# Columns of 1 + ca by one-column products, and one more pair of products of ones

## The chip, the cores and the metric

The kernel runs on one core of one Trainium2 chip. The metric is the device time of one execution in microseconds (us), the median of several runs. A core has TensorE (PE, with its weight loads listed apart as PEld), VectorE (DVE), ScalarE (ACT), GpSimd (POOL) and SyncE (SP), which here issues the DMAs. TensorE multiplies a loaded 128x128 block of weights with a stream of columns and writes into PSUM; the other engines read PSUM or SBUF.

## The reference

One block on x of 2048 rows by 512 columns, with a condition vector c of 512 numbers:

```python
mod = (silu(c) @ w_mod).reshape(1, 6, 1, -1)          # sa, ca, ga, sb, cb, gb: 512 numbers each
h = layernorm(x) * (1 + ca) + sa
x = x + ga * A(h)      # linear attention: 32 heads of 16, phi(q), phi(k), num / den, times wo
h = layernorm(x) * (1 + cb) + sb
x = x + gb * B(h)      # gelu(h @ w_in), halves z1 and z2, (w_sp @ layernorm(z2) + b_sp) * z1, times w_out
```

## The kernel before, in words

The rows are tiles of 128 (16 of them), the 512 columns four chunks of 128 (`KC`). Large products run on numbers split in two (`hi`, `lo`), three products for one. Three stages follow each other: q, k, v and the sums of the attention; the attention's output, the second layer norm and the gelu; and the product with w_sp, where seven products take the place of eight.

The order of all work is written out by hand as a string of short operation names with arguments (`ORDER`, `ORDER3`), and each engine takes its own instructions in that order. Which buffer a tile gets is written out too, as one digit for each allocation of a pool (`SLOTS`); a tile waits until the last user of its buffer is done.

The change is in the first few microseconds. There the layer norm's scale and shift are folded into the weights. For that the kernel needs 1 + ca in two forms. `col` (line 207) has it as one column for each chunk. `cbr` (line 326) has it divided by 512 and repeated along 128 columns, as the weights of a product that gives, for w_k and w_q, the mean of every column of the scaled weight matrix (`wm`, line 332). VectorE then forms the scaled weights less their mean (`wf`, line 336), ScalarE and VectorE or GpSimd split them (`wk`, `wq`, lines 340 and 343), and the first products of k (`kp`, line 417) start.

The operations at the start, in the order's names:

- `lm1,kc` loads chunk kc of w_mod for ca (`raw_mod`), `lw1,h` and `lw0,h` load the halves of w_k and w_q (`raw_qkv`), `ly` loads transposed x (`xt`); SyncE issues them all.
- `si` is silu(c) on ScalarE and VectorE: `sil`, 128x4.
- `du` is two products of a 128x128 tile of ones with itself (`warm`, line 172), whose result nobody reads.
- `cm1,kc` (`col_mm`) is four products with w_mod as weights and silu(c) as the streamed operand, into PSUM `pcol` (line 194).
- `mc` (`mean_col`) is ScalarE's copy from `pcol` to `cbr`; `ce1` (`col_end`) the one to `col`.
- `mr1,kc` and `mr0,kc` (`mean_mm`) are the mean products of w_k and w_q.

In the part that the diff leaves alone stands a product of another kind that the prediction uses: `col_part`, whose `pcol` (line 201) streams one column of ones.

Of the kernel before, what the change touches and what calls it, by code (L numbers as in the profile page):

```python
# [10 lines left out]
AF = mybir.ActivationFunctionType  # L11
# [3 lines left out]
P = 128  # L15
S, D, H, FH = 2048, 512, 32, 688
NT = S // P
KC = D // P
# [8 lines left out]
def block_kernel(ctx: ExitStack, tc: tile.TileContext, x, x_t, w_qkv, w_o, w_in, w_sp, b_sp, w_out,  # L27
                 w_out_tail, c, w_mod, ident_c, mask_c, out):
    nc = tc.nc

    def pool(name, bufs, space=None, stack=None):
        if space is None:
# [28 lines left out]
        "psb": "101010101010101010010101010101001010101",  # L61
        "zs": "0fe123d4cba9876523d483ca9473b2dca74b2dc724d9b7c9dbc9dbc9dbc90fe165d83a4270b9cfe8234",
        "tb": (
            "065412360541631520641326542362361232134614206320606346536132613136256106313012161350420435610253"
            "2564424054541321414101110331614101212465063563"
        ),
        "pst": "01011010101110101",
        "st": "032102312302102310232020312031320121302030132031231302032130210321032103132030211302210130132103",
        "ws": "0101",
        "pso": "010101001001110101011010110100101010010101010101",  # L70
        "tq": "nedc012mlba9876543kjgfihnea1m209ih60598l4k3bjca02inh16",
        "z1": "0000000000000000",
        "u": "0101101010101010",
        "c1": "0000000",
# [5 lines left out]
    def slot(tag):  # L80
        n = turn[tag] = turn.get(tag, -1) + 1
        return f"{tag}.{SLOTS[tag][n]}"

    def sb(tag, shape, dt, name):
        return pools[tag].tile(shape, dt, tag=slot(tag), name=name)

    def ps(kind, shape, name):
        return {"b": psb, "t": pst, "o": pso}[kind].tile(shape, F32, tag=slot("ps" + kind), name=name)
# [16 lines left out]
    mm = nc.tensor.matmul  # L105
# [30 lines left out]
    RAW = {}  # L136
# [37 lines left out]
    sil = const.tile([P, KC], F32, name="sil")  # L174
# [10 lines left out]
    MY, CP = {}, {}  # L185
# [2 lines left out]

    def col_mm(m, kc):
        if m not in CP:  # L190
            CP[m] = ps("t", [P, KC, P], f"pcol{m}")
        for i in range(KC):
            n = NCOL[m] = NCOL.get(m, 0) + 1
            mm(CP[m][:, i], RAW["mod", m, kc // 2][:, kc % 2, i * P:(i + 1) * P],
               sil[:, kc:kc + 1].to_broadcast([P, P]), start=n == 1, stop=n == KC * KC, skip_group_check=True)

    def col_part(key):
        CP[key] = ps("t", [P, KC], f"pcol{key}")
# [4 lines left out]

    def col_end(key):
        COL[key] = const.tile([P, KC], F32, name=f"col{key}")
        p = CP[key][:, :, 0] if key == 1 else CP[key]
        nc.scalar.activation(COL[key], p, AF.Copy, bias=1.0 if key == 1 else 0.0)

    def mod_vec(m, lo=0, hi=KC):
# [112 lines left out]
    WC, WF = {}, {}  # L322

    def mean_col():
        WC["c"] = sb("tb", [P, KC, P], F32, "cbr")
        nc.scalar.activation(WC["c"], CP[1], AF.Copy, scale=1.0 / D, bias=1.0 / D)

    def mean_mm(j, kc):
        if j not in WC:
# [208 lines left out]
    def win_lo(h, kc, eng=nc.gpsimd):  # L538
# [4 lines left out]
    OPS = {  # L543
        "lx": load_x, "lw": load_w, "lm": load_m, "li": load_ident, "du": lambda k: dummy(2), "si": silu,
        "ly": load_xt, "lk": load_wk, "s1": s1, "bh": s2_hi, "bl": s2_lo, "cm": col_mm, "cr": col_part, "ce": col_end,
        "mc": mean_col, "mr": mean_mm, "wf": w_mid,
        "cv": lambda: (col_part("v"), col_end("v")), "mv": lambda m, k: mod_vec(m, k, k + 1), "vp": v_prod, "va": v_add,
        "th": turn_hi, "tl": turn_lo,
        "by": bias_part, "bp": bias_prod, "ba": bias_add, "bx": bias_split, "bb": bias_row, "be": bias_end,
# [230 lines left out]
    def hx_lo(t):  # L780
# [13 lines left out]
        "l5": lambda: load_mod(5, "s4"),  # L794
    })
    ORDER = """
        lm1,0 lm1,1 si du1 du2 du3 du4 cm1,0 lm1,2 cm1,1 cm1,2 lm1,3 cm1,3 mc lw1,0 du5 mr1,0 mr1,1 ly1 th1
        tl1 ce1 lw1,1 mr1,2 mr1,3 ly0 th0 tl0 ly2 th2 wf1,3 qh1,3 qg1,3 lw0,0 tl2 lw0,1 wf1,1 mr0,0 mr0,1
        qh1,1 qg1,1 mr0,2 wf1,0 qh1,0 lx0 mr0,3 lm0,1 s10 yp0,1 ki1,3 ki1,1 lm0,0 yp0,0 ki0,3 ki0,1 ki0,0
        kj0,1 wf1,2 lm0,2 yp0,2 ki1,0 kj1,1 lm0,3 bh0 kj0,3 qh1,2 kj1,3 ki1,2 ly5 qd1,0 wf0,0 wf0,1 wf0,3  # L800
        ya0,1 kj1,0 yp0,3 ya0,2 ya0,3 ki0,2 qh0,1 qd1,2 th5 kj1,2 qh0,0 qg0,0 kj0,0 lx1 kj0,2 lx2 s12 bh2 cr0
# [380 lines left out]
```

## Time and profile before

| what | us |
|---|---|
| three runs | 619.77, 620.29, 621.38 |
| median | 620.29 |
| profiled execution | 620.6 |
| its span in the trace | 618.8 |

A fp32 product stands in the trace as two passes, each a weight load and a matmul; the written order counts products. A pass is shown from its issue to its modelled end, which lies behind the issue of the next one, so the pace is the distance between starts. In the timeline a row is: start, length, engine, line, operation, written tile <- read tiles, shapes, count, and in brackets the idle time ahead of it with what ended it. Rows that follow each other on an engine are merged. In the windows a row is: the stretch, its length, busy time of PE, PEld, DVE, ACT and POOL with the number of instructions, the granted clock of TensorE, the DMA share and GB/s.

### The profile page before, as it was taken

The numbers are of one execution on the slowest core, as the hardware profiler recorded it, in microseconds if no ns is written. First come the engines' busy times: TensorE is split into PE (matmuls) and PEld (weight loads), VectorE is DVE, ScalarE is ACT, GpSimd is POOL, SyncE is SP. The second block draws the span as 40 slices with busy tenths as digits, with TensorE's granted clock in tenths as the row PEclk, the third lists the DMA queues.
The fourth block names the chain that finished last, engine by engine and source line by source line (L and its number), as shares of the span: only waits on it lengthen the run. The fifth ranks groups of instructions, "written<-read, shape, count | busy, mean of one in ns | idle before, by whom it ended". The sixth has DMA issues, their size and how long they took to land.

```text
span 618.8 us, 9545 instructions
## 1 busy us (share of the span) xinstructions
PE 613.3 (99%) x3387; PEld 560.3 (91%) x3387; DVE 487.0 (79%) x902; ACT 336.1 (54%) x580; POOL 224.0 (36%) x185
## 2 busy tenths in 40 slices
PE   9999999999999999999999999999999999999997
PEld 6788888888899999999999999999999999998886
DVE  2999889897788878787786799997767787887661
ACT  2876767565656667565536464454354453544320
POOL 0843444637666576464252420132112111300000
PEclk9999999999999999999999999999999999999999
DMA  8463323261244667566844965552496555989962
GB/s 297 162 191 118 105 68 103 83 194 37 64 122 120 163 175 190 169 199 176 201 138 161 355 217 132 203 168 73 155 199 211 154 182 145 287 267 253 295 223 81
DMA packets 91022, 105.74 MB, mean 171 GB/s; under 512 B 57088, under 2 KB 57600, under 8 KB 90976
## 3 DMA queue, kind: packets, MB, share of 16 engines
q1 hardware_dynamic: 90976, 105.15, 57.2%
q8 instruction: 26, 0.43, 0.3%
q14 instruction: 20, 0.16, 0.1%
HBM read 66.07 MB, written 25.95 MB: 149 GB/s over the span
## 4 chain that ended last, share of the span: by engine, by line
PE 69%; DVE 14%; DMA 7%; issue 5%; POOL 2%; ACT 2%; SPq 1%; POOLq 0%; DVEq 0%; ACTq 0%
PE z L659 15%; PE P L937 13%; PE pout L111 3%; PE pout L112 3%; PE pout L110 3%; DMA raw_wsp<-in_w_sp 3%; PE g L110 2%; PE g L112 2%; PE qp L112 2%; PE qp L111 2%; PE qp L110 2%; PE g L111 2%; PE kp L110 2%; PE po L112 2%; PE kp L111 2%
## 5 line engine op out<-in xcount | busy, mean ns | idle before, releaser
L659 PE MATMUL z<-win,ht 128*128 128x344 f32 x768 | 123.0, 320 | 0.2 <-DVE ht L298 0.2
L659 PEld LDWEIGHTS z<-win,ht 128*128 128x128 f32 x768 | 121.4, 188 | 1.2 <-DVE ht L298 0.5
L937 PE MATMUL P<-z,f 128*128 128x344 f32 x624 | 103.3, 320 | 0.4 <-DVE f L927 0.4
L937 PEld LDWEIGHTS P<-z,f 128*128 128x128 f32 x624 | 99.1, 188 | 0.9 <-DVE f L927 0.7
L927 POOL TENSOR_TENSOR f<-raw_wsp,f 128x512 fp32r<-128x512 f32 x26 | 37.9, 1467 | 138.4 <-ACT f L924 132.1
L254 POOL TENSOR_TENSOR mv<-ve,mhalf 128x1 f32<-128x1 f32 x48 | 35.4, 740 | 54.9 <-DVE ve L253 52.5
L924 ACT ACTIVATE f<-raw_wsp 128x512 fp32r<-128x512 f32 x52 | 31.8, 626 | 29.9 <-PE P L937 14.1
L924 ACT ACTIVATE f<-sa 128x512 fp32r<-128x512 f32 x39 | 24.2, 629 | 33.2 <-DVE sa L914 10.1
L477 POOL TENSOR_TENSOR pksum<-pksum,tk 128x512 f32<-128x512 f32 x15 | 23.1, 1538 | 41.4 <-DVE tk L449 34.2
L927 DVE TENSOR_TENSOR f<-sa,f 128x512 fp32r<-128x512 f32 x39 | 28.5, 741 | 9.6 <-ACT f L924 9.6
L111 PE MATMUL pout<-wout,ut 128*128 128x512 f32 (+1 forms) x85 | 32.2, 379 | 0.2 <-DVE wout L1063 0.2
L110 PE MATMUL pout<-wout,ut 128*128 128x512 f32 (+1 forms) x85 | 32.2, 379 | 0.0
L112 PE MATMUL pout<-wout,ut 128*128 128x512 f32 (+1 forms) x85 | 32.2, 379 | 0.0
L695 POOL TENSOR_TENSOR z<-zz,z 128x688 fp32r<-128x688 f32 x16 | 29.2, 1842 | 7.5 <-ACT z L692 7.5
L937 PE MATMUL Pq<-z,wsp 128*128 128x344 f32 x192 | 30.8, 321 | 0.0
L937 PEld LDWEIGHTS Pq<-z,wsp 128*128 128x128 f32 x192 | 30.6, 188 | 0.0
L1032 ACT ACTIVATE ut<-ur 128x384 fp32r<-128x384 f32 x32 | 15.2, 518 | 24.8 <-DMA ur<-ud 15.8
L268 ACT COPY uca<-us 128x768 uint16<-128x768 uint16 x32 | 25.0, 828 | 5.3 <-PE P L937 3.6
L588 POOL TENSOR_TENSOR prod<-pq,zrep 128x512 f32<-128x512 f32 x16 | 21.7, 1370 | 14.5 <-ACT zrep L714 4.2
L110 PE MATMUL po<-m,pt 128*128 128x512 f32 x64 | 25.3, 396 | 0.0
L112 PE MATMUL po<-m,pt 128*128 128x512 f32 x64 | 25.3, 396 | 0.0
L110 PE MATMUL g<-pkhl,hhl 128*128 128x512 f32 x64 | 25.3, 395 | 0.0
(260 smaller groups left out, 1557.8 us busy)
## 6 DMA issues: line engine op xcount, KB each, us to landing
raw_wsp<-in_w_sp SPq DMA_DIRECT2D x32, 512.0 KB, 4.7
ud<-uca SPq DMA_DIRECT2D x16, 384.0 KB, 3.3
ur<-ud SPq DMA_DIRECT2D x16, 384.0 KB, 4.2
z1d<-z SPq DMA_DIRECT2D x16, 344.0 KB, 2.3
zd<-zz SPq DMA_DIRECT2D x16, 344.0 KB, 2.7
z1r<-z1d SPq DMA_DIRECT2D x16, 344.0 KB, 4.1
xt<-in_x_t SPq DMA_DIRECT2D x16, 256.0 KB, 3.0
x<-in_x SPq DMA_DIRECT2D x16, 256.0 KB, 2.9
```

The costliest lines, as they stand in the source:

```text
L110: mm(o, a_hi, b_hi, start=first, stop=False, **kw)
L111: mm(o, a_hi, b_lo, start=False, stop=False, **kw)
L112: mm(o, a_lo, b_hi, start=False, stop=last, **kw)
L254: nc.gpsimd.tensor_tensor(mv[:, 1:2], ve, mhalf, op=OP.pow)
L268: nc.scalar.copy(pl[:, h], v[:, :, h])
L477: nc.gpsimd.tensor_add(pksum, pksum, PK[t])
L588: nc.gpsimd.tensor_mul(pr, PQ[t], KV["z"])
L659: mm(p[:, b, :HB], a[:, i, kc], win[h][:, j, kc, b * HB:(b + 1) * HB], start=kc == 0 and k == 0, stop=kc == KC - 1 and k == 2)
L695: nc.gpsimd.tensor_sub(Z2[t][:, 1], ZZ[t], f(Z2[t][:, 0]))
L924: nc.scalar.activation(SF[p, h, k][:, 0], s_src(p, h, k), AF.Copy)
L927: eng.tensor_sub(SF[p, h, k][:, 1], s_src(p, h, k), f(SF[p, h, k][:, 0]))
L937: mm(B[key][:, :HB], a[:, x_], b[:, y_], start=i == 1, stop=i == n)
```

## The change

The 16 column products stream one column of silu(c) instead of the same column 128 times, and write a PSUM tile of 128x4 instead of 128x4x128. ScalarE's copy to `cbr` reads each of the four columns 128 times. In the order, `du6` is put behind `du5`: two more products of ones, four passes. In the buffer tables `tb` and `tq` a few digits change places (that of `tb`, two rows long, is left out below).

```diff
-            CP[m] = ps("t", [P, KC, P], f"pcol{m}")
+            CP[m] = ps("t", [P, KC], f"pcol{m}")
         for i in range(KC):
             n = NCOL[m] = NCOL.get(m, 0) + 1
-            mm(CP[m][:, i], RAW["mod", m, kc // 2][:, kc % 2, i * P:(i + 1) * P],
-               sil[:, kc:kc + 1].to_broadcast([P, P]), start=n == 1, stop=n == KC * KC, skip_group_check=True)
+            mm(CP[m][:, i:i + 1], RAW["mod", m, kc // 2][:, kc % 2, i * P:(i + 1) * P],
+               sil[:, kc:kc + 1], start=n == 1, stop=n == KC * KC, skip_group_check=True)
...
-        p = CP[key][:, :, 0] if key == 1 else CP[key]
+        p = CP[key]
         nc.scalar.activation(COL[key], p, AF.Copy, bias=1.0 if key == 1 else 0.0)
...
-        nc.scalar.activation(WC["c"], CP[1], AF.Copy, scale=1.0 / D, bias=1.0 / D)
+        nc.scalar.activation(WC["c"], CP[1][:, :, None].to_broadcast([P, KC, P]), AF.Copy, scale=1.0 / D, bias=1.0 / D)
...
-        "tq": "nedc012mlba9876543kjgfihnea1m209ih60598l4k3bjca02inh16",
+        "tq": "nedc012fgba9876543kjmlihnea1f209ih60598g4k3bjca02inh16",
...
-        lm1,0 lm1,1 si du1 du2 du3 du4 cm1,0 lm1,2 cm1,1 cm1,2 lm1,3 cm1,3 mc lw1,0 du5 mr1,0 mr1,1 ly1 th1
-        tl1 ce1 lw1,1 mr1,2 mr1,3 ly0 th0 tl0 ly2 th2 wf1,3 qh1,3 qg1,3 lw0,0 tl2 lw0,1 wf1,1 mr0,0 mr0,1
+        lm1,0 lm1,1 si du1 du2 du3 du4 cm1,0 lm1,2 cm1,1 cm1,2 lm1,3 cm1,3 mc lw1,0 du5 du6 mr1,0 mr1,1 ly1
+        th1 tl1 ce1 lw1,1 mr1,2 mr1,3 ly0 th0 tl0 ly2 th2 wf1,3 qh1,3 qg1,3 lw0,0 tl2 lw0,1 wf1,1 mr0,0 mr0,1
```

On TensorE the start of the program reads, before (a count is of products):

```order
L172 MATMUL warm<-ones 128x128 x8
L194 MATMUL pcol_182<-sil,raw_mod_0_166 128x128 x8
L194 MATMUL pcol_182<-sil,raw_mod_1_187 128x128 x8
L172 MATMUL warm<-ones 128x128 x2
L332 MATMUL wm_208<-raw_qkv_0_204,cbr 128x512 x2
L332 MATMUL wm_208<-raw_qkv_1_218,cbr 128x512 x2
L332 MATMUL wm_242<-raw_qkv_0_235,cbr 128x512 x2
```

And now:

```order
L172 MATMUL warm<-ones 128x128 x8
L194 MATMUL pcol_182<-sil,raw_mod_0_166 128x1 x8
L194 MATMUL pcol_182<-sil,raw_mod_1_187 128x1 x8
L172 MATMUL warm<-ones 128x128 x4
L332 MATMUL wm_210<-raw_qkv_0_204,cbr 128x512 x2
L332 MATMUL wm_210<-raw_qkv_1_220,cbr 128x512 x2
L332 MATMUL wm_244<-raw_qkv_0_237,cbr 128x512 x2
```

The two more products of ones stand ahead of the first mean products of w_k; the first `wm` is that of w_k, the second that of w_q. No other instruction has another place, on TensorE or on any other engine or queue. What the buffers' change moves is waits. On VectorE, where the scaled w_q is formed, before (with the engine or queue whose semaphore a row waits for):

```order
L343 TENSOR_TENSOR wk<-wf_248,wk 128x512 [waits Activation_49]
L336 SCALAR_TENSOR_TENSOR wf_303<-raw_qkv_0_235,col_216,wm_242 128x512 [waits DMAHW2_49,PE_49]
L336 SCALAR_TENSOR_TENSOR wf_305<-raw_qkv_0_235,col_216,wm_242 128x512 [waits Pool_49]
L336 SCALAR_TENSOR_TENSOR wf_307<-raw_qkv_1_238,col_216,wm_242 128x512 [waits DMAHW3_49,DVE_49]
L343 TENSOR_TENSOR wk<-wf_283,wk 128x512 [waits Activation_49]
```

And now:

```order
L343 TENSOR_TENSOR wk<-wf_250,wk 128x512 [waits Activation_49]
L336 SCALAR_TENSOR_TENSOR wf_305<-raw_qkv_0_237,col_218,wm_244 128x512 [waits DMAHW2_49,PE_49,Pool_49]
L336 SCALAR_TENSOR_TENSOR wf_307<-raw_qkv_0_237,col_218,wm_244 128x512
L336 SCALAR_TENSOR_TENSOR wf_309<-raw_qkv_1_240,col_218,wm_244 128x512 [waits DMAHW3_49,DVE_49]
L343 TENSOR_TENSOR wk<-wf_285,wk 128x512 [waits Activation_49]
```

The wait for GpSimd has moved up by one instruction, from `wf01` to `wf00`. The other changed pairs are `ek1` and `tk1` in the first stage, one z1 tile and one zz tile of the second, and buffers of `tq` in the third.

More of the change, by code (lines that the diff above doesn't have):

```diff
@@ L63, in block_kernel @@
         "tb": (
-            "065412360541631520641326542362361232134614206320606346536132613136256106313012161350420435610253"
-            "2564424054541321414101110331614101212465063563"
+            "065412365041631025641326042362361232134614256325656340630132013130260150313512101365425436015263"
+            "2604424654541321414161116331014161212405603503"
         ),
```

## Prediction

> **What bounds the kernel now.** I read the page first, then the chain of waits from its start, then the timeline of TensorE over the first 24 us, which is all that the change touches.
>
> ```profile
> PE 613.3 (99%) x3387; PEld 560.3 (91%) x3387; DVE 487.0 (79%) x902; ACT 336.1 (54%) x580; POOL 224.0 (36%) x185
> ...
> PE 69%; DVE 14%; DMA 7%; issue 5%; POOL 2%; ACT 2%; SPq 1%; POOLq 0%; DVEq 0%; ACTq 0%
> ```
>
> TensorE is busy for nearly the whole span and holds most of the chain. What is lost ahead of its long run of products therefore comes back as time, and the question is what sets the start of that run. The chain of waits in order of time says it (start, length, what):
>
> ```profile
> 5.67 8.57 DMA raw_qkv<-in_w_qkv
> 14.24 0.14 issue
> 14.38 3.67 PE wm L332 x8
> 18.05 5.58 PE kp L417 x24
> ```
>
> The first half of w_q lands at 14.24 and releases the mean products of w_q (`wm` at 14.38); right behind them come the first products of k (`kp`). What TensorE does before 14.38 is off the chain, as long as it is done by then. The timeline of the engines (start, length, engine, line, operation, count) shows what that is:
>
> ```profile
> 0.98 3.78 PE L172 MATMUL warm<-ones 128*128 128x128 f32 x16 [0.98 <-POOL tiny L124]
> 4.81 4.94 PE L194 MATMUL pcol<-sil,raw_mod 128*128 128x128 f32 x32
> 9.58 0.61 PE L172 MATMUL warm<-ones 128*128 128x128 f32 x4
> 9.78 0.60 ACT L326 ACTIVATE cbr<-pcol 128x512 f32<-128x512 f32 x1 [7.18 <-PE pcol L194]
> 10.43 3.70 PE L332 MATMUL wm<-raw_qkv,cbr 128*128 128x512 f32 x8 [0.24 <-ACT cbr L326]
> 14.38 3.67 PE L332 MATMUL wm<-raw_qkv,cbr 128*128 128x512 f32 x8 [0.24 <-DMA raw_qkv<-in_w_qkv]
> ```
>
> Each fp32 product is two passes in the trace, so two products per `du` are four passes. In order: 16 passes of ones, 32 column passes (`pcol`), 4 passes of ones beside ScalarE's copy `cbr`, 8 mean passes for w_k, 8 for w_q. The mean passes of w_k end at 14.13 by the row (10.43 + 3.70); with 0.592 us for a pass the last one starts at 13.54, and 0.429 later (their pace, below) TensorE could take the next, at 13.97. The slack before 14.38 is 0.4 us.
>
> The pace of the passes is the second thing to see. Three narrow windows of the timeline, with the tile view's lines for the two kinds of column passes behind them (min/median/max ns):
>
> ```profile
> 1.79 1.49 PE L172 MATMUL warm<-ones 128*128 128x128 f32 x6
> ...
> 5.58 1.70 PE L194 MATMUL pcol<-sil,raw_mod 128*128 128x128 f32 x7
> ...
> 7.80 1.39 PE L194 MATMUL pcol<-sil,raw_mod 128*128 128x128 f32 x11
> ...
> 11.82 1.88 PE L332 MATMUL wm<-raw_qkv,cbr 128*128 128x512 f32 x4
> ...
> L194 PEld LDWEIGHTS pcol<-sil,raw_mod x32: 190/191/333, 4.8 to 9.4; 128*128 128x128 f32 x32
> L194 PE MATMUL pcol<-sil,raw_mod x32: 273/273/554, 4.8 to 9.5; 128*128 128x128 f32 x32
> L201 PEld LDWEIGHTS pcol<-ones,yp x8: 187/192/192, 23.5 to 24.2; 128*128 128x128 f32 x8
> L201 PE MATMUL pcol<-ones,yp x8: 250/250/272, 23.5 to 24.3; 128*128 128x1 f32 x8
> ```
>
> A pass lasts longer than its distance to the next one, so I take the last pass off and divide by one less than the count. With 0.42 us for a slow pass, the second row gives (1.70 - 0.42) / 6 = 0.213 us; the third, with 0.273, gives 1.117 / 10 = 0.112; the fourth, with 0.592, 1.288 / 3 = 0.429. Passes of one form became 1.9 times as fast at about 7.2 us, in the middle of the `pcol` row, with no wait ended there. The granted clock stands in the windows at 1.00 from the start, so the opening has to be read from the durations; its closing does stand there:
>
> ```profile
> 614.00:616.00 2.00, 1.69 (x15) 1.48 (x13) 0.38 (x2) 0.00 (x0) 0.00 (x0) 1.00 0.19 66
> 616.00:618.00 2.00, 0.00 (x0) 0.00 (x0) 0.15 (x1) 0.00 (x0) 0.00 (x0) 1.00 0.19 66
> 618.00:618.80 0.80, 0.00 (x0) 0.00 (x0) 0.00 (x0) 0.00 (x0) 0.00 (x0) 0.60 0.00 0
> ```
>
> The last matmul ends at 615.69 (1.69 busy after 614.00). A mean of 0.60 over the last 0.80 us is 0.16 us at 1.0 and the rest at 0.5, so the clock fell at 618.16, about 2.5 us after the work stopped. TensorE thus begins at half speed, opened here 6.2 us after the first full-width pass (0.98 to 7.2), and answers idleness after 2.5 us.
>
> **The change part by part.** *One-column passes, if the clock is granted as before.* Each of the 32 passes streams 1 column where it streamed 128, but loads the same 128x128 weights. The kernel has such passes already:
>
> ```profile
> 23.47 1.05 PE L201 MATMUL pcol<-ones,yp 128*128 128x1 f32 x8
> ```
>
> (1.05 - 0.25) / 7 = 0.114 us apart, against 0.112 for the wide ones; the weight load bounds both (191 and 192 ns). So nothing is gained: the columns end at 9.6 or 9.7 as before. Even passes at no cost would gain nothing on the chain, since the 14.24 of w_q does not move: no DMA is moved, and the queue of SP has the same rows in the same order.
>
> *ScalarE's copy with a repeated source.* 128x512 written as before, at 0.60 us. The trace has no copy that reads one PSUM column 128 times. The nearest row is the copy itself; if it took twice as long, `cbr` would come at 10.98 and the w_k means would end 0.6 us later, 0.2 us past the slack. Faster by half would gain nothing. I take 0.
>
> *`du6`, four passes.* 4 x 0.112 = 0.45 us at full clock. The passes then run from 9.58 to 10.48, where `cbr` is there at 10.38 and the means began at 10.43: 0.05 us, inside the slack of 0.4. At half speed the eight take 8 x 0.213 = 1.7 us, and they stand ahead of the means on TensorE's queue.
>
> *Buffers.* In `tb` the tiles `wf00` and `wf01` change places, so that `wf00` now reuses the buffer whose last reader is GpSimd's second `wk` subtraction.
>
> ```profile
> 15.66 2.54 POOL L343 TENSOR_TENSOR wk<-wf,wk 128x512 fp32r<-128x512 f32 x2 [14.66 <-ACT wk L340]
> 19.08 2.06 DVE L336 SCALAR_TENSOR_TENSOR wf<-raw_qkv,col,wm 128x512 f32<-128x512 f32 x3
> ```
>
> That reader is done at 18.20 and `wf00` starts at 19.08: 0, with 0.9 us of cover. The other swaps in `tb` and `tq` are of pairs that follow each other closely; no engine's order moves. 0.
>
> *The clock, if one-column passes do not count toward it.* Between the ones that end at 4.56 and `du5`, TensorE would then do no work that the gate sees. The trace cannot price this directly: its only one-column stretch is 1 us long with the clock long open. I work it out from the rows above. The 32 passes stay at 0.213 (the slow weight load's 333 ns against 191 keeps that pace): 4.81 + 32 x 0.213 = 11.63. `du5` and `du6`: 1.7, to 13.33. `cbr` is done before that (last pass over at 11.84, plus 0.60 = 12.44). The w_k means start at 13.33 with a pass of 0.429 x 1.9 = 0.82 until the clock opens, 0.429 after. Full-width work began again at 11.63. The lower end for the opening is the gate's quick answer of 2.5 us, at 14.1; the upper end is the opening that the trace shows, 6.2 us, at 17.8. In the first case one pass is slow and seven are fast: the means end at 17.2. In the second 5.5 are slow: 18.9. The w_q means follow without a wait, as w_q has landed long before; against 14.38 that is +2.8 or +4.5 us. Where the gate stood in its cycle in this execution is one draw, so I take the middle, an opening at 16.0: 3.3 slow passes, 4.7 x 0.429 = 2.0, end at 18.0, **+3.7 us**.
>
> Nothing behind takes it back: the chain runs on from `wm` to `kp`, VectorE's `wf` and GpSimd's subtractions wait for the same means, and the later loads wait for buffers that these free. The 24 `kp` passes on the chain are 5.58 / 24 = 0.233 us apart, so there is no stall among them that could shrink in return.
>
> The Trainium skill, "TensorE: Matmul & The Clock Gate", Part 1 (The HAM clock gate), puts the gate's look at 3413 ns windows that run freely of the kernel; the trace agrees with that, 618.16 - 7.2 being 179.0 such windows. By that figure, as an estimate from the page, the first full window behind 11.63 ends 3.4 to 6.8 us later, which would give +3.2 to +4.8 us instead. The Trainium skill, the same page, Part 4 (PE-mode transpose), says that transposes do not count as PE-busy in the same way; no run here shows what a one-column pass counts as.
>
> Sum: 0 + 0 + 0 + 0 + 3.7. The profiled execution took 620.6 (span 618.8 and 1.8 around it), so 624.3. The median of the three runs is 620.29, 0.3 lower, and would give 624.0; I keep 624.3.
>
> **The rivals.**
>
> *The gate counts every pass.* Then the clock opens near 7.2 and all terms are 0 or hidden: 620.6, between 620.3 and 620.9. For it: TensorE and its weight load are both shown busy without a gap over one-column passes, and a weight load moves as much data as before. Against it: the array multiplies one column of 128. The point that decides is whether the 32 passes fall from 0.213 to 0.112 us within the `pcol` row. The Trainium skill, "TensorE: Matmul & The Clock Gate", Part 1, has the gate watch how busy TensorE is, which read plainly gives this case.
>
> *The gate opens early, on the first ones, and closes again.* The 16 passes of ones last 3.6 us; with another position of the gate's cycle that may do. The columns then run fast, the clock falls before the means, and opens again between 13 and 15 us: w_k's means from 10.4 have 3.2 to 5.6 slow passes and end between 15.1 and 16.0, +0.7 to +1.6 us, some 621.8. Against it: in this execution the ones alone did not open it.
>
> *Faster.* Columns that end early would let w_k's means start when w_k lands. But w_q's landing at 14.24 holds what follows, and behind it stand only the 0.14 us of issue: 620.5 at best. To pass 0.3%, w_q's means would have to start at 12.5, before their data are there. Only an effect far behind that I do not see, of the swapped buffers, does that.
>
> **How the numbers follow.** The clock withheld: 0.55. Every pass counts: 0.28. Opens and closes again: 0.10. Faster: 0.07. A measurement of this kernel tells about 0.3% (1.9 us) from no change. Slower is the first case and a third of the third, 0.58; same is the second with the rest of the third, 0.35; faster 0.07. The likeliest case alone spans 623.1 to 625.1. Since the second and third cases hold too much to leave out, the range reaches down to them, and half a microsecond further for the scatter of the runs shown (619.77 to 621.38): 619.8 to 625.4.
>
> **What would show it.** Right: `pcol` passes 0.21 us apart to the end, `pcol` over near 11.6, eight passes of ones to 13.3, the first means 0.8 us apart, w_q's means starting between 17 and 19 with no DMA wait, and the chain at the start running over TensorE instead of w_q's transfer. Wrong: passes 0.11 us apart after some 7 us and `wm` for w_q still at 14.4. What would upset all of it is a wait that the buffer swaps add far behind, or a slow repeated copy of well over 1 us.

## The result, and the profile after

The changed kernel takes 626.50 us (median of 8 runs, 622.35 to 627.27) against 620.33 of the kernel before beside it: a ratio of 1.0081, 95% interval 1.0063 to 1.0099. It is slower, by 5.0 us (3.9 to 6.1) as the ratio gives it; the medians alone lie 6.2 us apart. Its runs spread over 5 us where those of before spread over 1.7. The profiled execution is one of the quicker ones: 624.17, span 622.0.

The page after shows where in the span the clock is missing. These are its first slices of the granted clock, and the chain by engine:

```profile
PE 616.0 (99%) x3391; PEld 561.8 (90%) x3391; DVE 487.7 (78%) x902; ACT 335.6 (54%) x580; POOL 223.2 (36%) x185
...
PEclk7999999999999999999999999999999999999999
...
PE 83%; DVE 5%; DMA 5%; issue 3%; POOL 2%; ACT 1%; SPq 0%; POOLq 0%; DVEq 0%; ACTq 0%
```

The first slice has seven tenths; before, it read nine. The timeline of TensorE and ScalarE's copy, after (start, length, engine, line, operation, count):

```profile
4.79 1.92 PE L194 MATMUL pcol<-sil,raw_mod 128*128 128x1 f32 x16
6.88 2.48 PE L194 MATMUL pcol<-sil,raw_mod 128*128 128x1 f32 x16 [0.17 <-DMA raw_mod<-in_w_mod]
9.22 2.06 PE L172 MATMUL warm<-ones 128*128 128x128 f32 x8
9.40 0.60 ACT L326 ACTIVATE cbr<-pcol 128x512 f32<-128x512 f32 x1 [6.79 <-PE pcol L194]
11.07 8.95 PE L332 MATMUL wm<-raw_qkv,cbr 128*128 128x512 f32 x16
```

And the windows of the same execution (stretch, length, busy PE, PEld, DVE, ACT, POOL, granted clock, DMA share, GB/s):

```profile
4.70:8.00 3.30, 3.10 (x27) 2.98 (x27) 0.00 (x0) 0.00 (x0) 0.00 (x0) 1.00 0.89 258
8.20:14.80 6.60, 6.60 (x19) 4.53 (x20) 1.39 (x2) 2.55 (x5) 0.00 (x0) 0.50 1.03 405
15.00:20.00 5.00, 5.00 (x13) 2.23 (x12) 3.34 (x6) 1.93 (x4) 1.88 (x2) 1.00 1.02 385
```

Here the ones alone opened the clock: the first 16 one-column passes already come (1.92 - 0.25) / 15 = 0.111 us apart. Then it fell while TensorE was busy with one-column passes, between 8.0 and 8.2, and came back between 14.8 and 15.0. The 16 mean passes follow each other without a break, since w_q has long landed. The last ends at 20.02 where it was 18.05 (14.38 + 3.67) before: 2.0 us. The repeated copy takes 0.60 us as before.

That is not the whole loss. If each product of TensorE is laid beside the same product of before, the delay is 2.4 to 2.5 us from 26 us on and stays so until 380 us; it is 4.2 at 385 and 3.2 at the end. The step lies in the third stage, where the change reaches only by buffer numbers. Windows at that place, before and then after:

```profile
380.00:390.00 10.00, 10.00 (x65) 10.00 (x65) 9.09 (x20) 3.78 (x8) 2.55 (x2) 1.00 0.84 228
```

```profile
380.00:390.00 10.00, 8.87 (x54) 8.29 (x53) 9.86 (x21) 5.64 (x11) 0.19 (x1) 1.00 0.57 151
```

TensorE, busy without a gap before, lacks 1.1 us of work there, and VectorE is now the engine with hardly a gap. In the waits from 340 to 400 us, before and then after, TensorE waits for VectorE's `f`:

```profile
PE P L937 <- DVE f L927: 0.2, 1, 0.2
```

```profile
PE P L937 <- DVE f L927: 1.0, 1, 1.0
```

VectorE in turn starts on the tiles `e` late, before and then after:

```profile
346.79 1.98 DVE L873 TENSOR_TENSOR e<-e 128x344 f32<-128x344 f32 x1
```

```profile
351.92 0.52 DVE L873 TENSOR_TENSOR e<-e 128x344 f32<-128x344 f32 x1 [2.60 <-DMA e<-zd]
```

SyncE's queue shows why these tiles come late. Before:

```profile
342.68 0.32 SPq L688 DMA_DIRECT2D zd<-zz  x1
343.10 0.38 SPq L868 DMA_DIRECT2D e<-zd  x1
343.53 0.45 SPq L868 DMA_DIRECT2D o<-zd  x1
```

After:

```profile
345.14 0.32 SPq L688 DMA_DIRECT2D zd<-zz  x1
348.80 0.32 SPq L868 DMA_DIRECT2D e<-zd  x1
349.17 0.42 SPq L868 DMA_DIRECT2D o<-zd  x1
```

The first load of `e` (the third stage's z tiles) comes 0.42 us behind the last store of `zz` before, and 3.66 us behind it after.

So there are two theories. The clock theory: one-column passes do not count toward TensorE's clock. The buffer theory: the swapped tables hold back the loads of the third stage. Rivals are that the four more passes are the loss (queue theory), and that the step at 380 us only follows from the shift at the start.

### The profile page after: what moved, and what is told of

It is laid out like the page before. It is cut to its first block, busy times and chain, and to the rows that moved or that the text cites. A ratio compares the mean times of both kernels' runs of the same rounds, so it can differ in the third digit from the quotient of the medians.

```text
span 622.0 us, 9549 instructions
## 1 busy us (share of the span) xinstructions
PE 616.0 (99%) x3391; PEld 561.8 (90%) x3391; DVE 487.7 (78%) x902; ACT 335.6 (54%) x580; POOL 223.2 (36%) x185
## 4 chain that ended last, share of the span: by engine, by line
PE 83%; DVE 5%; DMA 5%; issue 3%; POOL 2%; ACT 1%; SPq 0%; POOLq 0%; DVEq 0%; ACTq 0%
PE P L937 22%; PE z L659 16%; PE Pq L937 5%; PE pout L111 3%; PE pout L110 3%; PE pout L112 3%; PE g L110 2%; PE g L112 2%; PE qp L112 2%; PE qp L111 2%; PE qp L110 2%; PE g L111 2%; PE kp L110 2%; PE po L112 2%; PE kp L111 2%
```

## The experiments

**Wide products again, all else as changed.**

```diff
-            CP[m] = ps("t", [P, KC], f"pcol{m}")
+            CP[m] = ps("t", [P, KC, 128], f"pcol{m}")
...
-               sil[:, kc:kc + 1], start=n == 1, ...
+               sil[:, kc:kc + 1].to_broadcast([P, 128]), start=n == 1, ...
...
-        nc.scalar.activation(WC["c"], CP[1][:, :, None].to_broadcast([P, KC, P]), ...
+        nc.scalar.activation(WC["c"], CP[1][:, :, 0:1].to_broadcast([P, KC, P]), ...
```

> Everything of the change but the narrow products: the column products stream 128 columns again, ScalarE still copies one of them 128 times, du6 and the swapped buffer tables stay. Clock theory (one-column passes do not count toward TensorE's clock): no loss is left, 620.3 as before, within 0.7 us; the pace doubles once near 4.7 to 8 us and the clock stays open; w_q's means start near 14.4. Buffer theory (part of the loss, the 0.7 to 1.2 us that the changed kernel's trace shows from 381 us on, is from the swapped tables): 621.0 to 621.5, with that step at 381 us again. Queue theory (the four more passes are the loss): 624 to 627.

Measured: 623.11, ratio 1.0034 (1.0018 to 1.0049), 2.1 us. The start of its timeline:

```profile
4.60 4.91 PE L194 MATMUL pcol<-sil,raw_mod 128*128 128x128 f32 x32
9.34 1.05 PE L172 MATMUL warm<-ones 128*128 128x128 f32 x8
10.23 3.66 PE L332 MATMUL wm<-raw_qkv,cbr 128*128 128x512 f32 x8
14.46 2.81 PE L332 MATMUL wm<-raw_qkv,cbr 128*128 128x512 f32 x6 [0.57 <-DMA raw_qkv<-in_w_qkv]
```

The start is whole again: w_q's means wait for w_q. `du6` and the copy are hidden, as the prediction had them. But 2.1 us are lost, and TensorE's delay, under 0.3 us up to 380, is 1.7 us at 385. Neither the clock theory alone (620.3) nor the queue theory (624 to 627) has that; the buffer theory has, with about twice its number (0.7 to 1.2 us).

**Narrow products and copy alone**, with du5 alone and the tables of before.

```diff
-        ... cm1,3 mc lw1,0 du5 du6 mr1,0 mr1,1 ly1
+        ... cm1,3 mc lw1,0 du5 mr1,0 mr1,1 ly1
...  the tables tb and tq as before the change
```

> The narrow products and the repeated copy alone: no du6, the buffer tables of before. Clock theory: the loss stays, 622 to 627 with a median 0.4 to 0.9 us under the changed kernel's, since four slow passes (0.85 us) are gone ahead of w_k's means but the clock opens no earlier. Buffer theory: 1 us or more under the changed kernel's. Queue theory: 620.3 as before.

Measured: 623.75, ratio 1.0050 (1.0032 to 1.0068), 3.1 us. The queue theory falls. The loss without the tables is 2 us under that of the whole change, more than the four passes explain.

**64 columns in place of one.** The first diff with 64.

> The changed kernel with 64 streamed columns in place of 1 (128 before); the weight load still sets the pace, so the passes come at the same distance. If the clock goes by the time in which the array is streamed through, a pass counts half here: either that is enough (620.3, pace doubled once and kept) or it is not (622 to 627, as with one column). I expect it not to be enough to open the clock but enough to keep it open, so some runs near 620.3 and some near 625. If the loss had nothing to do with the streamed share, the time is the changed kernel's.

Measured: 627.47, ratio 1.0082 (1.0053 to 1.0111), but in two groups: 623.10 to 623.64 in three runs, 627.47 to 628.14 in four. That is the mix expected. The quicker group is 2.3 to 2.8 us above the 620.83 of the kernel before beside it, about what the tables cost (below). The trace is of the second group and shows all 32 passes at the slow pace, (7.06 - 0.42) / 31 = 0.214 us:

```profile
4.73 7.06 PE L194 MATMUL pcol<-sil,raw_mod 128*128 128x64 f32 x32
11.58 2.02 PE L172 MATMUL warm<-ones 128*128 128x128 f32 x8
13.39 4.73 PE L332 MATMUL wm<-raw_qkv,cbr 128*128 128x512 f32 x7
```

That the first group had its clock opened by the ones and kept is inferred from the times, and from the mean granted clock on record for each run, which shows no fall in any of the seven (0.999 or 1.0); no trace of it was taken.

**The changed kernel once more.**

> The changed kernel as it is, for further draws of the clock's position. Clock theory: 622 to 627, and in the trace the delay of w_q's means against 14.4 us follows from when the clock opens: 2.0 us where it opened early, fell and opened again at 14.9, up to 4.6 where it opens once, at 17 to 18 us. What the time is beyond that delay arises behind 26 us.

Measured: 627.06 (624.71 to 627.67), ratio 1.0092 (1.0066 to 1.0117). In this trace the clock had another position:

```profile
4.67 6.96 PE L194 MATMUL pcol<-sil,raw_mod 128*128 128x1 f32 x32
11.48 2.05 PE L172 MATMUL warm<-ones 128*128 128x128 f32 x8
13.33 4.16 PE L332 MATMUL wm<-raw_qkv,cbr 128*128 128x512 f32 x6
```

All 32 passes are slow, (6.96 - 0.35) / 31 = 0.213 us, and w_k's means start at 13.33. The granted clock does not show this, as in the trace of before: it stands at 1.00 until its first change.

```profile
4.70:16.00 11.30, 11.30 (x45) 9.75 (x45) 1.38 (x2) 2.44 (x5) 0.00 (x0) 1.00 1.00 359
```

TensorE's delay is 3.7 us at the last mean pass (13.33 + 8.45 = 21.78 against 18.05), 4.2 from 26 us on, and 5.5 to 6.1 from 385 on.

So the mean granted clock of a run tells which of the two happened: a clock that opens early and falls takes about 0.005 off it (6.6 us at 0.50, of 622), one that opens late takes nothing off. By that, the clock opened early and fell in six of the eight runs of the result (0.994 to 0.997), and in 22 of the 39 runs of all forms with one-column passes at the start; the others, and the runs of the kernel before whose clock is listed, stand at 0.999 or 1.0.

**The swapped tables alone**, in the kernel before.

```diff
-            "065412360541631520641326542362361232134614206320606346536132613136256106313012161350420435610253"
+            "065412365041631025641326042362361232134614256325656340630132013130260150313512101365425436015263"
...
-        "tq": "nedc012mlba9876543kjgfihnea1m209ih60598l4k3bjca02inh16",
+        "tq": "nedc012fgba9876543kjmlihnea1f209ih60598g4k3bjca02inh16",
```

> The kernel before with the swapped buffer tables alone. Buffer theory, now with its place: after the swap the first load of e (the third stage's z tiles) stands on SyncE's queue behind a wait for the store of the last zz tile, which was issued just before; so it is issued 3.5 us after that store where 0.4 us was enough, and eight loads behind it come as late. 622.0 to 622.7, 1.3 to 2.1 us over the kernel before, all of it arising at about 380 us, nothing before. If the step in the earlier runs was from the shift of the start alone, 620.5 as before.

Measured: 623.62, ratio 1.0037 (1.0023 to 1.0051), 2.3 us. The start is nearly undisturbed (0.3 us), the delay is 1.7 at 385 us. SyncE's queue and TensorE's window:

```profile
343.01 0.32 SPq L688 DMA_DIRECT2D zd<-zz  x1
346.69 0.32 SPq L868 DMA_DIRECT2D e<-zd  x1
```

```profile
380.00:390.00 10.00, 9.17 (x57) 8.60 (x56) 9.79 (x22) 4.13 (x9) 2.55 (x2) 1.00 0.72 181
```

3.68 us between store and load, with nothing shifted at the start. The written order names the wait. Before the change the seventh of these loads waits for DMAHW2, the semaphore of the last `zz` store; with the tables it is the first:

```
L688 DMA zd_3968<-zz_3619 128x688 [waits DMAHW2_49,Activation_49]
L868 DMA e_3998<-zd_3249 128x688 [waits DMAHW3_49,DMAHW2_49,Pool_49]
L868 DMA o_3999<-zd_3077 128x688 [waits DMAHW4_49]
```

Some of the third stage's `tq` buffers lie over the `tb` buffers of the stages before it. The swap of the digits 0 and 6 brought zz_14, whose store is the last, under the buffer of the first load. So that load now waits for all that still reads zz_14: the store, and GpSimd's subtraction `z` (line 695; the wait for `Pool`, which before the change was for an earlier instruction). The waits of SyncE's queue from 342 to 349 us in this run give both:

```profile
SPq L868 <- DMA zd<-zz: 1.9, 1, 1.9
SPq L868 <- POOL z L695: 1.4, 1, 1.4
```

The store ends first. The subtraction ends last, at 346.67 (344.97 + 1.70), and the load is issued at 346.69. The loads of this queue are issued one behind the other (`o` 0.37 us after `e`), so every load behind the first is late too.

**The changed kernel with the tables of before.**

```diff
...  the tables tb and tq as before the change; narrow products, copy and du6 stay
```

> The changed kernel with the buffer tables of before: narrow products, repeated copy, du6. Clock theory and buffer theory as two separate terms: 1.5 to 2 us under the changed kernel's 626 to 627, so 624 to 625, spread from 621.5 to 625.5 by the clock's position; no step at 380 us. If the two are one effect, as much as the changed kernel.

Measured: 624.46 (623.12 to 626.87), ratio 1.0053 (1.0033 to 1.0072), 3.3 us. Two terms, then, that add: 3.3 for the clock and 2.3 for the tables, against 5.0 to 5.7 for both. The profiled run was the slowest of the seven: it has 4.3 us of delay after the start, as a clock that opens late gives, and gains 1.8 more between 390 and 530 us, though TensorE has no gap at 380 to 390. What that is stays open.

**du6 alone**, in the kernel before.

```diff
-        ... cm1,3 mc lw1,0 du5 mr1,0 ...
+        ... cm1,3 mc lw1,0 du5 du6 mr1,0 ...
```

> The kernel before with du6 alone. Clock theory: the four passes cost 0.45 us at full clock inside the slack ahead of w_q's landing, so 620.5 as before, within 0.5. If the passes ahead of w_k's means are a loss of their own, 0.5 to 0.9 us more.

Measured: 621.54, ratio 1.0011 (0.9999 to 1.0023): no difference that can be told.

**Added stretches in mid-kernel**, which measure the disputed rule by itself. Their results are not used.

```diff
+    def stretch(w, n):
+        ...
+        for _ in range(n):
+            mm(p[:, :w], f(ones), f(ones[:, :w]), start=True, stop=True)
...
+        ... kh3 qa0 xx1,70 k44 ...   and  gm6 xx32,70 km11   and  gm10 xx64,70 q412
```

> The kernel before with three added stretches of 70 products of ones (140 passes, about 16 us each at full pace, 47 us together, results unused) far inside the first stage, where the clock has long been open: the first streams 1 column, the second 32, the third 64. The weight load keeps TensorE busy all the time in each. Clock theory: in the first the granted clock falls to 0.5 within about 3.4 to 7 us, the passes go from 0.11 to 0.21 us apart, and it comes back 3.4 to 7 us after the stretch. In the second and third it falls or holds as the streamed share (a quarter, a half) is under or over the gate's bound; by the spread of the 64-column run I expect it to fall at 32 and to hold at 64. If every pass counts, it holds in all three.

Measured: 693.08. The windows around the stretches of 1 and 32 columns, then the 64-column stretch in the timeline:

```profile
60.00:64.00 4.00, 4.00 (x38) 3.96 (x36) 3.50 (x9) 3.93 (x7) 1.74 (x2) 1.00 0.86 285
64.30:86.00 21.70, 21.70 (x104) 21.70 (x103) 1.55 (x5) 3.04 (x6) 2.70 (x3) 0.50 0.00 1
...
91.60:95.00 3.40, 3.40 (x16) 2.76 (x15) 0.57 (x1) 0.00 (x0) 0.00 (x0) 1.00 0.00 0
119.00:122.00 3.00, 3.00 (x28) 2.96 (x26) 2.56 (x7) 2.79 (x5) 1.56 (x2) 1.00 0.00 0
122.30:146.00 23.70, 23.70 (x113) 23.70 (x113) 0.00 (x0) 1.84 (x3) 0.96 (x1) 0.50 0.04 11
...
184.00:199.00 15.00, 15.00 (x137) 15.00 (x136) 2.24 (x4) 2.12 (x4) 1.69 (x1) 1.00 0.26 94
```

```profile
183.91 15.74 PE L179 MATMUL str<-ones 128*128 128x64 f32 x140
```

With TensorE and its weight load both shown busy for 21.70 of 21.70 us, the clock stood at 0.50: it fell 4 us after one-column passes began and came back only behind them. At 32 columns it fell in the same way; at 64 it held. The rival "every pass counts" is out. The Trainium skill, "TensorE: Matmul & The Clock Gate", Part 1 (The HAM clock gate), has the gate watch how busy TensorE is. Busy as the profile counts it does not decide here: TensorE is shown busy without a gap in all three stretches, and the clock fell with 1 and with 32 streamed columns and held with 64.

**The tables with two buffers exchanged**, in the kernel before.

```diff
-        "tq": "nedc012fgba9876543kjmlihnea1f209ih60598g4k3bjca02inh16",
+        "tq": "aedc012fgbn9876543kjmlihaen1f209ih60598g4k3bjcn02iah16",
```

> The kernel before with the swapped buffer tables, and in the table of the third stage the buffers n and a exchanged throughout. That puts the wait for the store of the last zz tile from the first load of e on SyncE's queue back to the seventh of the eight, where it stood before the change. Buffer theory: the loss of the tables alone (1.0037) is gone, 620.5 to 621.2, and the first load of e is issued 0.4 us after the store. If it was another of the swapped buffers, or the tables' places themselves, 623 to 624 as with the tables alone.

Measured: 620.94, ratio 1.0003 (0.9990 to 1.0016). The loss is gone, with the load 0.41 us behind the store and TensorE's window full:

```profile
342.70 0.32 SPq L688 DMA_DIRECT2D zd<-zz  x1
343.11 0.38 SPq L868 DMA_DIRECT2D e<-zd  x1
```

```profile
380.00:390.00 10.00, 10.00 (x66) 10.00 (x65) 9.51 (x20) 3.93 (x9) 2.55 (x2) 1.00 0.85 234
```

**The changed kernel with the same exchange.** The same line in the changed kernel.

> The changed kernel with the same exchange of n and a. Two separate terms: 1.5 to 2.3 us under the changed kernel, 624 to 624.5, what is left being the clock's. If the exchange does nothing, 626 to 627.

Measured: 623.73, ratio 1.0055 (1.0037 to 1.0073), as with the tables of before. What is left is the clock's.

**96 columns**, with the tables of before and du6.

> The changed kernel with the buffer tables of before and 96 streamed columns, three quarters of a full pass. The run with 64 columns did not open the clock in its trace. If the gate asks for nearly full streaming to open, 623 to 625 and an opening at 14 us or later in the trace; if three quarters are enough, 620.5 to 621.5 and an opening between 4 and 8 us.

Measured: 620.99, ratio 1.0007 (0.9990 to 1.0023): no loss that can be told. The 32 passes of its trace take 4.73 us where 64 columns took 7.06:

```profile
4.75 4.73 PE L194 MATMUL pcol<-sil,raw_mod 128*128 128x96 f32 x32
```

With three quarters of a full pass the clock opened within these passes, and none of the ten runs was late; with a half it did not open in the trace that was taken. But it opened about 2 us into them (some ten passes are slow), so the full passes of ones just ahead can have helped: 96 columns alone were not tested. No variant was told faster than the kernel before: where the clock opened in time, w_q's landing held the start.

## Why the prediction was right, and where it was wrong

- **What bounds the start** (w_q's landing at 14.24, 0.4 us of slack ahead of it): right. Where the clock opened in time, w_q's means started at 14.2 to 14.8 and waited for that DMA, whatever stood before them.
- **One-column passes are no faster**, the weight load sets the pace: right, 0.213 and 0.112 us at one column as at 128.
- **The copy and du6 at nothing**: right, 0.60 us for the copy; du6 alone 1.0011 with 1 inside the interval.
- **The clock, +3.7 us between 2.8 and 4.5**: the step that decided it, and right as a mechanism. Alone it costs 3.1 to 3.4 us in three forms (1.0050, 1.0053, 1.0055). The trace of the second set of runs has the case as it was worked out: passes 0.213 us apart to the end, w_k's means from 13.33 and 0.85 us apart, 3.7 us at the last mean. Of the signs named for it the first trace has two alone, the first means 0.85 us apart and no wait for w_q. The chain at the start, which was to run over TensorE, runs over loads, ScalarE's `yp` and GpSimd's `yp` in both.
- **Opens early and closes again**, a rival at 0.10, is what that first trace shows, and what six of the eight runs of the result had. So its chance was far too low, judged from one trace in which the ones alone did not open the clock. It was mis-sized too: 0.7 to 1.6 us were worked out, and it was 2.0 at the means, as the clock came back at the late end of its range (15) and w_k's means started at 11.07, not 10.4: the eight passes of ones ran at half speed, which the rival had left out. It rests on the same rule as the first case, with the clock at another position.
- **Luck in the size**: in the three forms without the tables' loss, the 14 runs whose clock opened early lie on average 2.5 us over the median of the kernel before, the 11 others 4.0. The 3.1 to 3.4 is a mix of the two, and that 3.7 lies near it is luck in part.
- **Nothing behind takes it back**: right, but 0.4 to 0.5 us came on top, behind the means, along that chain. VectorE's first `wf` waits for the means of w_k, not of w_q, and starts 2.46 us late in the first trace (16.63 against 14.17); GpSimd's `yp` and the `pcol` of line 201 come as much later. The slack of 0.4 us ahead of w_q's means does not cover that path.
- **Buffers at 0**: wrong, and the one term of the sum that failed. The prediction looked at the first stage's swap (the wait of `wf00` for GpSimd, indeed hidden) and set the other swaps to 0 because pairs that follow each other closely change places. The runs showed 2.3 us (1.0023 to 1.0051): the tables also decide which old buffer lies under a buffer of the next stage, and the new waits fell on the head of a queue. The prediction named "a wait that the buffer swaps add far behind" among what would upset it, and gave it no price.
- **Total**: 3.7 predicted, 5.0 measured (3.9 to 6.1). The two terms by themselves, 3.3 and 2.3, make 5.6, inside that interval. On the 620.29 of before the ratio gives 625.3, just under the range's upper end of 625.4, and the median of the changed kernel's own runs, 626.50, is over it. That the total stayed within the range is luck: the buffers' 2.3 us were missing, and the clock cost less than the case that was worked out, which came to 4.2 us behind the means.

## What to carry to other kernels

A pass that streams few columns (1 or 32 of 128 here) keeps TensorE busy in the profile, 21.70 of 21.70 us, and lets its clock fall to 0.50; before narrowing a product that the weight load paces anyway, look at what share of columns the passes around it stream. One trace shows one position of the clock: the mean clock of every run told how often each case came. Where buffers are assigned by table, compare the waits at the head of each DMA queue in every stage, not only around the edit: here two waits that fell on the first of eight loads cost 2.3 us.

## What the runs showed that was not expected

The clock seems to have two bounds, where the prediction thought of one. To hold it, 64 of 128 columns were enough and 32 were not; to open it, 64 were not enough. That is one trace each, with ones streamed in the first and silu(c) in the second. And a passing burst of full work can open it for one short stretch only to be followed by a closed one: the changed kernel's trace has 1.00, 0.50 and 1.00 within its first 15 us.
